# Reordering the softmax chunks and the scores of an attention and feed-forward kernel

## The chip, the core and the metric

The kernel runs as one program on one core of a Trainium2 chip. The metric is the device time of one execution in microseconds (us), as the median over the runs shown. Below, PE is TensorE (the matmuls), PEld its weight loads, DVE is VectorE, ACT is ScalarE, POOL is GpSimd and SP is SyncE, which issues most of the DMAs.

## What is computed

The inputs are x (2048 tokens of 512 numbers), the weights of a sliding-window attention with 32 heads of 16 numbers, and those of a gated feed-forward layer with 1792 hidden units. The reference, cut to what matters:

```
xn = layernorm(x)
q, k, v = split(xn @ wqkv)                       # 32 heads, 16 numbers each
mask = (0 <= idx[:, None] - idx[None, :] < 256)  # each token sees itself and 255 before it
p = softmax(where(mask, q k^T * 16**-0.5, -1e9))
s = (p v) @ wo
g = silu((silu(xn @ w1) * (xn @ w3)) @ w2)
return x + s * g
```

The kernel takes the maximum of every row first and subtracts it before the exponential. Products of two f32 matrices are made as three f16 products (high by high, low by high, high by low).

## The kernel before, in words

**Stages.** Tokens go in four tiles `t` of 512. Heads go in four groups `g` of eight, and a group in two halves `p` of four heads. A `(t, g, p)` is a unit; there are 32, and the outer loop (L1157) walks through them. In a unit PE makes, interleaved, four kinds of work:

- `pass1` (L542): scores with the queries on the partitions, eight parts for a unit (four blocks of 128 queries, two pairs of heads). Each writes one scores tile `s` (matmuls of L558), and DVE takes the maximum of each row (L568). It runs two units ahead of `pass2`. A unit's maxima are turned by two small matmuls (`finish`, L583) that write into spare columns of another part's scores tile, and go through a DMA into two rows of `qa`.
- `pass2` (L608): scores again, with the keys on the partitions and the maxima subtracted in the matmul (L629). This is done in chunks; the tuple `CHUNKS` (L64) lists them for tiles 1 to 3, `FIRST` (L70) for tile 0. A piece `(m, k, n, at, used)` is 64 keys from block `m` against `n` blocks of 64 queries. DVE adds masks (L636) and ACT takes the exponential into a tile `pt` (L639). The first two chunks of `CHUNKS` have 8 blocks of queries for each half of the keys and for one pair of heads each (`a` = 0, then 1), as pieces of 5 and 3; the next two the same in pieces of 5, 2 and 1; the last one has 4 blocks for both pairs of heads.
- the products with v (`values`, L643, L655): f32 matmuls of 64 rows by 32 columns, so that eight fit into the array beside each other (two halves of the keys by four heads). They come in two calls for a unit of tiles 1 to 3: chunks 0, 1, 2 and then chunks 3, 4 (`cuts`, L987). The two last units, which have no `pass1` beside them, make three calls: (0, 1), (2, 3) and (4).
- dense work: projections (L504), values (L471), the two products of the feed-forward layer (`gate_up` L797, `down` L842) and the output (L884). Each group of 9 or 12 matmuls fills one bank `m0` or `m1`, in two halves; the two banks alternate, and DVE or ACT empties a bank when its group is complete.

**What sets the order.** PE's order is the order of the program; the other engines' orders are made by the scheduler, with `urgent()` pieces ahead. `batches` (L981) lists the scores of a unit, `pass2`'s and `pass1`'s in turn, and takes them two at a time as a batch; after the two scores of a batch come the products with v that the batch before made ready (`late`). `spread` (L1015) puts dense pieces between the batches. A unit of tiles 1 to 3 has 5 + 8 = 13 scores, so one is carried into the next unit: in every other unit each batch has the weights' scores (`pass2`) first, in the ones between the maxima's scores (`pass1`) first. Scores tiles `s` come from a pool of two buffers; a buffer is free again when DVE has the maxima, or ACT the exponentials.

**Delayed steps.** `later(n, f)` runs `f` after `n` steps; a step is one dense piece or one batch. `later_in_bank` (L151) does the same for pieces that use a bank for a moment, but only in the middle of an open dense group (`pump`, L157), and takes the bank that is not open (`bank(short=True)`, L170).

**Scaling weights.** In tile 0 the raw weights are scaled to powers of two. `squares` (L221) sums squares on ACT and DVE, `powers` (L249) adds them over the partitions with a matmul with ones (L255) into such a bank, and DVE makes the power of two from it. Then `split` or `split_pool` cut the weights into f16 halves on ACT, DVE and POOL. `measure` (L737) does it for two slices of the feed-forward weights at once.

**The next tile's x.** `prepare_beside(t)` (L445) loads four blocks of x, takes their means and variances on DVE (`stats`, L371, from 8 steps later on), centres them, and turns them with small matmuls into spare columns of `pass1`'s scores tiles (`turn_beside`, L418, from the list `besides`).

Of the kernel before, what the change touches and what calls it, by code (L numbers as in the profile page):

```python
# [76 lines left out]
def tile_block(ctx: ExitStack, tc: tile.TileContext, x, wqkv, wo, w1, w3, w2, out):  # L77
# [50 lines left out]
    queue = []  # L128
    banked = []
    started = []  # L130
# [19 lines left out]

    def later_in_bank(n, f):  # L151


        made_so_far[0] += 1
        banked.append((now[0] + n, made_so_far[0], f))

    def pump():  # L157
        due = min((q for q in banked if q[0] <= now[0]), default=None)
        if due is not None:
            banked.remove(due)  # L160
            due[2]()

    def flush():
        while queue or banked:
            step()
            pump()

    open_bank = [0]

    def bank(shape, dtype=F32, short=False):  # L170

        b = 1 - open_bank[0]
        if not short:
            open_bank[0] = b
        return psm.tile(shape, dtype, name=f"m{b}", tag=f"m{b}", bufs=1)


# [70 lines left out]

    def powers(sb, n, p2, inv):  # L249


        ps = bank([P, n], short=True) if started else pss.tile([P, 2, 512], F32, name="s")[:, 0, 0:n]
        m = sb.shape[-1] // n
        for i in range(m):
            nc.tensor.matmul(ps, onesb, sb[:, i * n:(i + 1) * n], start=i == 0, stop=i == m - 1)  # L255
        al = small.tile([P, n], F32, name="al")
        nc.vector.tensor_scalar(al, ps, 2.08, 1e-30, op0=ALU.mult, op1=ALU.max)

        nc.vector.tensor_scalar(al.bitcast(I32), al.bitcast(I32), 24, 23, op0=ALU.logical_shift_right,
                                op1=ALU.logical_shift_left)  # L260
        nc.vector.tensor_scalar(p2, al, 2.0**63, None, op0=ALU.mult)
        nc.vector.reciprocal(inv, p2)

# [23 lines left out]
    def weights(name, w):  # L287

        cell = {}

        def load():
            cell["raw"] = [take(F32) for _ in range(NC)]
            for c, raw in enumerate(cell["raw"]):
                nc.sync.dma_start(raw, w[c * P:(c + 1) * P, :])

        def norm(apart=0):
            cell["sb"] = squares(cell["raw"], on_act=2 * (name == "wv"), apart=apart)

        def scale():
            p2 = const.tile([P, 1], F32, name=f"p2{name}")  # L300
            inv = const.tile([P, 1], F32, name=f"inv{name}")
            powers(cell["sb"], 1, p2, inv)
            cell["p2"], cell["inv"], cell["sw"] = p2, inv, scaled(inv, WS, f"sw{name}")

        def cut(apart=0):
            hi = const.tile([P, NC, D], F16, name=f"{name}h")
            lo = const.tile([P, NC, D], F16, name=f"{name}l")

            def one(c, raw):
                split(hi[:, c, :], lo[:, c, :], raw, cell["sw"])  # L310
                give(raw)
            for c, raw in enumerate(cell["raw"]):
                if apart:
                    later(apart * c, lambda c=c, raw=raw: one(c, raw))
                else:
                    one(c, raw)
            SQ[name] = hi, lo, cell["p2"], cell["inv"]
        return load, norm, scale, cut

    def weights_qk(g):  # L320
# [10 lines left out]

        def scale():
            p2 = const.tile([P, 1], F32, name=f"p2qk{g}")
            inv = const.tile([P, 1], F32, name=f"invqk{g}")
            powers(cell["sb"], 1, p2, inv)
            cell["p2"], cell["sw"] = p2, scaled(inv, WS, f"sw{g}")

# [23 lines left out]
    def prepare(t):  # L361
# [32 lines left out]
        def turn(b):  # L394
# [9 lines left out]
            else:  # L404
                pt = pss.tile([P, 2, 512], F32, name="s")[:, 0, :].rearrange("p (k q) -> p k q", q=P)
            for k in range(NC):
# [37 lines left out]

    def prepare_beside(t):  # L445

# [3 lines left out]
        for b in range(4):  # L450
            made.append((0, lambda b=b: later(8 + b, lambda: stats(b))))
        made.append((0, lambda: later(12, lambda: rstd(0, 4))))
        for b in range(4):
            made.append((0, lambda b=b: later(13 + b, lambda: centre(b))))
        return made, lambda: besides.extend(lambda s, b=b, n=n: turn(b, n, s) for b in range(4) for n in (0, 2))
# [22 lines left out]


    maxima = []  # L480
    besides = []
    QA = {}
# [59 lines left out]
    def pass1(t, g, p):  # L542
# [6 lines left out]
        def part(ii, a):  # L549
            qa, ka = QA[t, g], keys(t, g)  # L550
            i = t * 4 + ii
            n, mask = ((i + 1) * P, M1.rearrange("p a b -> p (a b)")[:, (1 - i) * P:]) if i < 2 else (WIN, MW)
            s = pss.tile([P, 2, 512], F32, name="s")
            for c in range(2):
                e = (ii + 3) * P if i < 2 else (ii + 2) * P + 64 * (c + 1)
                for r in range(2):
                    rows = slice(64 * r, 64 * r + KR)
                    nc.tensor.matmul(s[64 * c:64 * c + 64, r, :n], qa[rows, 2 * p + a, ii * P + 64 * c:ii * P + 64 * c + 64],  # L558
                                     ka[rows, 2 * p + a, e - n:e], start=True, stop=True)
# [38 lines left out]
    def last_maxima():  # L598
        s = pss.tile([P, 2, 512], F32, name="s")
        after = [f(s) for f in maxima]  # L600
# [7 lines left out]
    def pass2(t, g, p, cuts):  # L608
# [14 lines left out]
        def scores(c):  # L623
            qa, ka = QA[t, g], keys(t, g)
            s = pss.tile([P, 2, 512], F32, name="s")
            for o, h, a, (m, k, n, _, _) in pieces(c):
# [110 lines left out]
    def measure(f, apart=0):  # L737
# [3 lines left out]

        def scale():
            pp = small.tile([P, 3, 2], F32, name="pp")
            pi = small.tile([P, 3, 2], F32, name="pi")
            powers(sb, 6, pp.rearrange("p a b -> p (a b)"), pi.rearrange("p a b -> p (a b)"))
            ff = slice(f, f + 2)
# [234 lines left out]
    def batches(n, u, ahead):  # L981
# [9 lines left out]
        if u and not ahead and maxima:  # L991
            order.append((last_maxima, None))
        for k in range(max(len(rows1), len(rows2))):
            order += [(f, c) for f, c in zip(rows2[k:k + 1], cols2[k:k + 1])]
            order += [(f, None) for f in rows1[k:k + 1]]
        if len(order) % 2 and n < len(units) - 1:
# [3 lines left out]
        due = late_cost[0]  # L1000
        for pair in pairs:
            def batch(pair=pair):
                for f, _ in pair:
                    f()
                ready = late[:]
                late.clear()
                late.extend(c[1] for _, c in pair if c)
                for c in ready:
                    c()
            made.append((due, batch))  # L1010
            due = sum(COLS * c[0] for _, c in pair if c)
        late_cost[0] = due
        return made

    def spread(made, dense):  # L1015
# [4 lines left out]
        for k, (cost, batch) in enumerate(made):  # L1020
# [3 lines left out]
            while dense and (at + dense[0][0] / 2 <= whole * (k + 1) / len(made) or dense[0][0] == 0):  # L1024
                c, piece = dense.pop(0)
                at += c
                piece()
                if is_open([(c, piece)]):
                    pump()
                if c:  # L1030
# [3 lines left out]
    def run(dense):  # L1034
        for c, piece in dense:
            piece()
            if started and is_open([(c, piece)]):
                pump()
            if c:
# [32 lines left out]
    def keep_busy(n):  # L1072
        ps = bank([P, 4, P], short=True)
        for _ in range(n):
# [58 lines left out]
    later_in_bank(3, lambda: (qk[3][2](), later(2, qk[3][3])))  # L1133
    spread(batches(-1, None, units[1]), project(0, 2, 1) + project(0, 2, 0) + more(EARLY))

# [21 lines left out]
    for n, u in enumerate(units):  # L1157
        if n == 1:
            first, second = prepare_beside(1)
            run(first)  # L1160
            later(22, second)
        if n == 6:
            wout[0]()
        if n == 7:
            wout[1](2)
            later_in_bank(12, lambda: (wout[2](), later(2, lambda: wout[3](2)), later(3, out_scale)))
        want += a_unit - other[n]
# [8 lines left out]
    while late:  # L1176
# [4 lines left out]
        step()  # L1181
    while banked:
        step()
        pump()
    for b in range(2):
# [33 lines left out]
```

## Time and profile before

| | |
|---|---|
| median of 3 runs | 899.93 us (899.12 to 901.4) |
| the profiled execution | 900.77 us |
| its span, first to last instruction | 898.7 us |
| mean granted clock of TensorE | 0.992 of full speed |
| instructions in the span | 22393 |

The profiled execution took 2.07 us more than its span; this lies before the first and after the last instruction. Line numbers are those of the kernel before. In a line of the timeline the first number is the start in us from the start of the span, the second how long the group of equal instructions lasted, `x` how many there were, and the bracket how long the engine was idle before and who ended it. A matmul's listed end is modelled and reaches over the start of the next one, so distances are taken from start to start. In a line of the waits the numbers are us in total, how many times, and the longest.

### The profile page before, as it was taken

How to read it: one execution, taken by the hardware profiler on the slowest of the kernel's cores; microseconds unless marked ns; L12 is line 12 of the kernel's file. 1: busy time of each engine (PE TensorE's matmuls, PEld its weight loads, DVE VectorE, ACT ScalarE, POOL GpSimd, SP SyncE). 2: the span in 40 equal slices, each digit the busy share in tenths (PEclk: the TensorE clock that was granted, in tenths of full speed). 3: DMA queues.
4: the chain of work that ended last, by engine and by line, in shares of the span. 5: the costliest groups of instructions: out<-in, count | busy, mean ns of one | idle time of the engine just before them, and what ended most of it. 6: DMA issues, size and time to landing. Idle time of an engine off the chain costs nothing.

```text
span 898.7 us, 22393 instructions
## 1 busy us (share of the span) xinstructions
PE 848.7 (94%) x8695; PEld 391.5 (44%) x8695; DVE 613.2 (68%) x2009; ACT 407.4 (45%) x594; POOL 193.4 (22%) x317
## 2 busy tenths in 40 slices
PE   9797997889999999999999999999999999999997
PEld 4333443344444444444445444444444444444443
DVE  8676777766787676787668675766566676666435
ACT  6895866573425444233343444443343334442521
POOL 2244236251101102121111111121111112121211
PEclk9999899999999999999999999999999999999999
DMA  9865434547443344442432334333343243332301
GB/s 302 260 203 156 148 126 131 183 113 225 119 135 84 97 135 131 115 130 74 145 100 72 108 105 149 112 114 84 98 123 93 78 132 113 98 119 58 88 8 59
DMA packets 95322, 110.61 MB, mean 123 GB/s; under 512 B 17200, under 2 KB 60528, under 8 KB 95216
## 3 DMA queue, kind: packets, MB, share of 16 engines
q1 hardware_dynamic: 94928, 108.67, 41.0%
q8 instruction: 68, 1.11, 0.5%
q10 hardware_dynamic: 288, 0.52, 0.2%
q14 instruction: 38, 0.31, 0.1%
HBM read 76.28 MB, written 28.57 MB: 117 GB/s over the span
## 4 chain that ended last, share of the span: by engine, by line
PE 52%; DVE 15%; DMA 10%; issue 9%; ACT 7%; SPq 4%; POOL 3%; POOLq 0%; ACTq 0%; DVEq 0%
PE m L797 19%; PE m L842 9%; PE po L655 8%; DVE junk L568 5%; ACT pt L639 5%; PE m L504 3%; PE s L558 3%; DVE s L636 3%; PE s L629 3%; DMA slot<-in_B_w_dram 3%; PE m L471 3%; PE m L884 3%; POOL slot L276 2%; DMA dr<-dd 2%; SPq L702 2%
## 5 line engine op out<-in xcount | busy, mean ns | idle before, releaser
L639 ACT ACTIVATE pt<-s,es 128x1024 f32<-128x1024 f32 x152 | 169.1, 1115 | 252.2 <-DVE s L636 226.9
L568 DVE CUSTOM_DVE_ANT_0 junk<-s,MW 128x320 bf16<-128x320 f32 x448 | 217.9, 486 | 78.1 <-PE s L558 56.7
L797 PE MATMUL m<-XH,slot 128*128 128x512 f16 x896 | 268.7, 382 | 1.9 <-DVE slot L517 1.9
L276 POOL TENSOR_TENSOR slot<-slot,slot 128x256 f16<-128x256 f32 (+1 forms) x220 | 144.4, 681 | 543.7 <-ACT slot L821 391.0
L797 PEld LDWEIGHTS <-slot 128*128 128x128 f16 x1344 | 122.9, 98 | 155.2 <-issue 13.7
L797 PE MATMUL m<-XL,slot 128*128 128x512 f16 x448 | 170.3, 380 | 0.0
L842 PE MATMUL m<-slot,slot 128*128 128x512 f16 x672 | 157.6, 383 | 1.6 <-DVE slot L812 1.2
L636 DVE TENSOR_TENSOR s<-s,MK 128x256 f32<-128x256 f32 (+2 forms) x280 | 121.3, 435 | 40.9 <-PE s L629 37.0
L655 PE MATMUL po<-pt,V 64*32 64x320 f32 (+4 forms) x2880 | 100.8, 348 | 0.0
L842 PEld LDWEIGHTS <-slot 128*128 128x128 f16 x672 | 61.8, 98 | 83.1 <-issue 12.7
L558 PE MATMUL s<-KA,qa 48*64 48x320 f16 (+2 forms) x1024 | 73.3, 304 | 15.4 <-ACT pt L639 8.5
L655 PEld LDWEIGHTS po<-pt,V 64*32 64x32 f32 x2880 | 62.3, 106 | 34.1 <-issue 15.5
L629 PE MATMUL s<-qa,KA 50*64 50x320 f16 (+3 forms) x1472 | 61.7, 258 | 12.0 <-ACT pt L639 10.8
L629 PEld LDWEIGHTS <-KA 50*64 50x64 f16 x1472 | 37.1, 105 | 57.1 <-issue 37.1
L808 ACT ACTIVATE slot<-m,sgs 128x512 f32<-128x512 f32 x56 | 38.4, 686 | 50.2 <-PE m L797 49.0
L812 DVE SCALAR_TENSOR_TENSOR slot<-slot,m 128x512 f32<-128x512 f32 x56 | 38.4, 686 | 31.0 <-ACT slot L808 27.9
L817 DVE SCALAR_TENSOR_TENSOR slot<-m,slot 128x512 f32<-128x512 f32 x56 | 38.4, 685 | 29.2 <-PE m L797 28.9
L558 PEld LDWEIGHTS <-qa 48*64 48x64 f16 x1024 | 28.3, 105 | 67.2 <-issue 42.4
L821 ACT CAST slot<-slot 128x512 f16<-128x512 f32 x56 | 34.6, 617 | 47.4 <-DVE slot L817 46.8
L858 DVE SCALAR_TENSOR_TENSOR slot<-m,dsc,slot 128x512 f32<-128x512 f32 x48 | 35.9, 747 | 22.0 <-PE m L842 21.4
L276 POOL TENSOR_TENSOR on<-on,rb 128x256 f32<-128x256 f32 x32 | 23.0, 741 | 129.3 <-DMA dm<-mt 47.0
L504 PE MATMUL m<-XH,whi 128*128 128x512 f16 x120 | 44.8, 381 | 0.2 <-DVE slot L812 0.2
(143 smaller groups left out, 849.0 us busy)
## 6 DMA issues: line engine op xcount, KB each, us to landing
slot<-dW SPq DMA_DIRECT2D x126, 256.0 KB
slot<-in_B_w_dram SPq DMA_DIRECT2D x42, 256.0 KB
dW<-slot SPq DMA_DIRECT2D x42, 256.0 KB
slot<-in_A_x_dram SPq DMA_DIRECT2D x30, 256.0 KB
KA<-dK SPq DMA_DIRECT2D x24, 288.0 KB
qa<-dQ SPq DMA_DIRECT2D x32, 192.0 KB
dK<-slot SPq DMA_DIRECT2D x16, 256.0 KB
dQ<-slot SPq DMA_DIRECT2D x16, 256.0 KB
```

The source lines that it names most:

```text
L276: op(out[:, c], a[:, c], b[:, c])
L504: nc.tensor.matmul(cell["pp"], a[:, k, c, :], b[:, c, :], start=(c, i) == parts[0][0], stop=(c, i) == parts[-1][-1])
L558: nc.tensor.matmul(s[64 * c:64 * c + 64, r, :n], qa[rows, 2 * p + a, ii * P + 64 * c:ii * P + 64 * c + 64], ka[rows, 2 * p + a, e - n:e], ...
L568: nc.vector.tensor_tensor_reduce(out=junk[:, :n], in0=s[:, r, :n], in1=mask, scale=1.0, scalar=NEG, op0=ALU.add, op1=ALU.max, accum_out=M[ ...
L629: nc.tensor.matmul(s[64 * h:64 * h + 64, r, o:o + 64 * n], ka[rows, 2 * p + a, 64 * (m + 4):64 * (m + 5)], qa[rows, 2 * p + a, 64 * (m + k ...
L636: nc.vector.tensor_add(v, v, MK[:, kind, of:of + n, :].unsqueeze(1).to_broadcast([P, 2 * len(which), n, 64]))
L639: nc.scalar.activation(pt, s, AF.Exp, scale=es)
L655: nc.tensor.matmul(cell["po"][32 * i:32 * i + 32, h, 64 * (m + k):64 * (m + k + n)], V[64 * h:64 * h + 64, (4 * t + m // 2) % VB, hd * VW: ...
L797: nc.tensor.matmul(cell[k], w[:, (a * NC + c) * P:(a * NC + c + 1) * P], b[:, c, :], start=c == 0 and i == 0, stop=c == NC - 1 and i == 2)
L808: nc.scalar.activation(sg, cell[0], AF.Tanh, scale=sg_scale[:, f:f + 1])
L812: nc.vector.scalar_tensor_tensor(sg, sg, 1.0, cell[0], op0=ALU.add, op1=ALU.mult)
L842: nc.tensor.matmul(ps, hh[:, a * TW + b * P:a * TW + (b + 1) * P], w[:, c * D:(c + 1) * D], start=f == f0 and i == 0, stop=f == f1 - 1 and ...
```

## The change

Five things change together.

1. `CHUNKS`: the chunk of all four heads moves from the last to the first place. `cuts` stays, so for a unit of tiles 1 to 3 the first call of `values` now has that chunk and the two of pieces 5 and 3, and the second call the two of pieces 5, 2 and 1.
2. In every batch the weights' scores come first (`pair.sort`).
3. The matmuls with ones no longer use a dense bank. `powers` takes a scores tile of `pass1` and writes, as four 64 by 64 products, into its spare columns; a list `besides` says which part does it (`beside_scores`, in front of the turns of x). `later_in_bank`, `pump` and `short` go. DVE adds the two halves with one instruction more.
4. At most one part of a batch carries something in its spare columns (`alone`), save in tile 0 and the first group of tile 1.
5. For tile 1, `prepare_beside` does its statistics 6 steps later and gives the turns free after 26 steps in place of 22, and one projection (keys of tile 1, group 0) goes a unit later.

```diff
-CHUNKS = (*((a, ((0, 0, 5, 0, 1), (-2, 2, 3, 5, 1)), ((1, 0, 5, 0, 1), (5, 0, 3, 5, 1)),
+CHUNKS = (((0, 1), ((4, 0, 4, 0, 1),), ((-1, 1, 4, 0, 1),), ((0, 3, 2, 2, 0),)),
+          *((a, ((0, 0, 5, 0, 1), (-2, 2, 3, 5, 1)), ((1, 0, 5, 0, 1), (5, 0, 3, 5, 1)),
              ((0, 4, 2, 0, 0), (5, 2, 2, 1, 0))) for a in AB),
           *((a, ((2, 0, 5, 0, 1), (6, 0, 2, 5, 1), (-4, 4, 1, 7, 1)), ((3, 0, 5, 0, 1), (7, 0, 1, 5, 1), (-3, 3, 2, 6, 1)),
-             ((0, 4, 2, 0, 0), (5, 2, 2, 0, 0))) for a in AB),
-          ((0, 1), ((4, 0, 4, 0, 1),), ((-1, 1, 4, 0, 1),), ((0, 3, 2, 2, 0),)))
+             ((0, 4, 2, 0, 0), (5, 2, 2, 0, 0))) for a in AB))
...
-    def bank(shape, dtype=F32, short=False):
-
-        b = 1 - open_bank[0]
-        if not short:
-            open_bank[0] = b
+    def bank(shape, dtype=F32):
+
+        open_bank[0] = b = 1 - open_bank[0]
         return psm.tile(shape, dtype, name=f"m{b}", tag=f"m{b}", bufs=1)
...
+    def beside_scores(n, f):
+
+        later(n, lambda: besides.insert(0, f))
...
-    def powers(sb, n, p2, inv):
+    def powers(sb, n, p2, inv, s=None):
...
-        ps = bank([P, n], short=True) if started else pss.tile([P, 2, 512], F32, name="s")[:, 0, 0:n]
         m = sb.shape[-1] // n
-        for i in range(m):
-            nc.tensor.matmul(ps, onesb, sb[:, i * n:(i + 1) * n], start=i == 0, stop=i == m - 1)
...
+            for h in range(2):
+                for c in range(2):
+                    for i in range(m):
+                        nc.tensor.matmul(s[64 * c:64 * c + 64, h, WIN:WIN + n],
+                                         onesb[64 * h:64 * h + 64, 64 * c:64 * c + 64],
+                                         sb[64 * h:64 * h + 64, i * n:(i + 1) * n], start=i == 0, stop=i == m - 1)
...
-            made.append((0, lambda b=b: later(8 + b, lambda: stats(b))))
-        made.append((0, lambda: later(12, lambda: rstd(0, 4))))
+            made.append((0, lambda b=b: later(more + 8 + b, lambda: stats(b))))
+        made.append((0, lambda: later(more + 12, lambda: rstd(0, 4))))
...
-            after = [f(s) for f in maxima if (ii, a) != (0, 0)]
-            if after:
+            after = []
+            if alone[0] and maxima and (ii, a) != (0, 0):
+                after = [f(s) for f in maxima]
                 maxima.clear()
-            elif besides:
+            elif alone[0] and besides:
                 after = [besides.pop(0)(s)]
+            alone[0] = not after or t * NG + g <= NG
...
-        (later_in_bank if started else later)(5 if started else 9 if apart else 6, scale)
+        if started:
+            beside_scores(4, scale)
+        else:
+            later(9 if apart else 6, scale)
...
         for pair in pairs:
+
+            pair.sort(key=lambda x: x[2])
+
             def batch(pair=pair):
-                for f, _ in pair:
+                alone[0] = True
+                for f, _, _ in pair:
                     f()
...
-    later_in_bank(1, lambda: (qk[2][2](), later(1, qk[2][3])))
+    beside_scores(4, lambda s: then(s, qk[2][2](s), lambda: later(1, qk[2][3])))
...
-            if max(2 * k - 5, 0) == n:
+            if max(2 * k - 5 + (k == NG), 0) == n:
                 beside[n] += project(*tiles[k], 1)
...
-            first, second = prepare_beside(1)
+            first, second = prepare_beside(1, 6)
             run(first)
-            later(22, second)
+            later(26, second)
```

More of the change, by code (lines that the diff above doesn't have):

```diff
@@ L149, in step, with scores_bank @@
             due[2]()
[L151 to L161, printed above, removed]
     def flush():
-        while queue or banked:
+        while queue:
             step()
-            pump()
     open_bank = [0]
-    def bank(shape, dtype=F32, short=False):
-        b = 1 - open_bank[0]
-        if not short:
-            open_bank[0] = b
+    def bank(shape, dtype=F32):
+        open_bank[0] = b = 1 - open_bank[0]
         return psm.tile(shape, dtype, name=f"m{b}", tag=f"m{b}", bufs=1)
+    def scores_bank():
+        return pss.tile([P, 2, 512], F32, name="s")
+    maxima = []
+    besides = []
+    alone = [True]
+    def beside_scores(n, f):
+        later(n, lambda: besides.insert(0, f))
     identf = const.tile([P, P], F32, name="identf")
@@ L330, in norm, with scale, rest @@
             cell["sb"] = squares(cell["raw"], on_act=2)
-        def scale():
+        def scale(s=None):
             p2 = const.tile([P, 1], F32, name=f"p2qk{g}")
             inv = const.tile([P, 1], F32, name=f"invqk{g}")
-            powers(cell["sb"], 1, p2, inv)
-            cell["p2"], cell["sw"] = p2, scaled(inv, WS, f"sw{g}")
+            def rest():
+                cell["p2"], cell["sw"] = p2, scaled(inv, WS, f"sw{g}")
+            return then(s, powers(cell["sb"], 1, p2, inv, s), rest)
         def cut(ks=(1, 0)):
@@ L404, in turn @@
             else:
[L405 removed]
+                pt = scores_bank()[:, 0, :].rearrange("p (k q) -> p k q", q=P)
             for k in range(NC):
@@ L598, in last_maxima @@
     def last_maxima():
-        s = pss.tile([P, 2, 512], F32, name="s")
+        s = scores_bank()
         after = [f(s) for f in maxima]
@@ L624, in scores @@
             qa, ka = QA[t, g], keys(t, g)
-            s = pss.tile([P, 2, 512], F32, name="s")
+            s = scores_bank()
             for o, h, a, (m, k, n, _, _) in pieces(c):
@@ L1006, in batch @@
                 late.clear()
-                late.extend(c[1] for _, c in pair if c)
+                late.extend(c[1] for _, c, _ in pair if c)
                 for c in ready:
@@ L1010, in batches @@
             made.append((due, batch))
-            due = sum(COLS * c[0] for _, c in pair if c)
+            due = sum(COLS * c[0] for _, c, _ in pair if c)
         late_cost[0] = due
@@ L1072, in keep_busy @@
     def keep_busy(n):
-        ps = bank([P, 4, P], short=True)
+        ps = bank([P, 4, P])
         for _ in range(n):
@@ L1165, in tile_block @@
             wout[1](2)
-            later_in_bank(12, lambda: (wout[2](), later(2, lambda: wout[3](2)), later(3, out_scale)))
+            beside_scores(12, lambda s: then(s, wout[2](s), lambda: later(2, lambda: wout[3](2)), lambda: later(3, out_scale)))
         want += a_unit - other[n]
```

64 lines of the change are left out of this document (37 added, 27 removed).

## The prediction

> **What bounds the kernel now.** First the span on the profile's page, then busy time by stage (0:285 is tile 0, 285:830 tiles 1 to 3 with both passes side by side, 830 on the end).
>
> ```profile
> span 898.7 us, 22393 instructions
> ```
>
> ```profile
> 0.00:285.00 285.00, 257.35 (x2441) 115.90 (x2445) 209.62 (x776) 174.79 (x307) 89.68 (x163) 0.98 0.56 170
> 285.00:830.00 545.00, 527.69 (x5722) 246.04 (x5726) 372.17 (x1181) 211.93 (x260) 91.34 (x136) 1.00 0.37 108
> 830.00:898.70 68.70, 63.71 (x544) 29.51 (x536) 31.42 (x54) 20.65 (x27) 12.37 (x18) 0.99 0.18 51
> ```
>
> The columns behind the length are PE, PEld, DVE, ACT and POOL. In the middle stage PE is busy 527.69 of 545 us; DVE, the next engine, 372.17, or 68%. What is taken off PE there shortens the kernel almost one for one, and about 17 us of idle PE are the most that better order can win. In the first stage PE is idle 27.65 us (285 less 257.35), so there a wait can be won, but other engines are late as well. What PE waits for, by stage (middle first, then the first):
>
> ```profile
> PE s L629 <- ACT pt L639: 9.5, 19, 1.3
> PE s L558 <- ACT pt L639: 4.6, 8, 1.3
> ```
>
> ```profile
> PE m L255 <- DVE sb L242: 4.3, 1, 4.3
> PE m L255 <- DVE slot L817: 4.3, 1, 4.3
> PE m L255 <- DVE slot L812: 1.7, 1, 1.7
> PE m L255 <- DVE slot L517: 0.8, 1, 0.8
> ```
>
> In the middle the scores wait for the exponential that frees their tile; in tile 0 the largest waits stand before the products with ones (L255). The change touches all three: PE's products with v, the scores' waits, the products with ones.
>
> **Step 1, the chunks.** The timeline of PE shows the products with v of the first and the last unit whose calls are (0, 1, 2) and (3, 4), there being 22 such units (24 units of tiles 1 to 3 less the last two), each with the start of the next work:
>
> ```profile
> 288.58 1.96 PE L655 MATMUL po<-pt,V 64*32 64x320 f32 x56
> 290.48 0.39 PE L797 MATMUL m<-XH,slot 128*128 128x512 f16 x1
> ...
> 295.45 1.53 PE L655 MATMUL po<-pt,V 64*32 64x320 f32 x40
> 296.91 0.39 PE L797 MATMUL m<-XH,slot 128*128 128x512 f16 x1
> ...
> 809.28 1.96 PE L655 MATMUL po<-pt,V 64*32 64x320 f32 x56
> 811.17 0.39 PE L797 MATMUL m<-XH,slot 128*128 128x512 f16 x1
> ...
> 816.63 1.53 PE L655 MATMUL po<-pt,V 64*32 64x320 f32 x40
> 818.09 0.39 PE L797 MATMUL m<-XH,slot 128*128 128x512 f16 x1
> ```
>
> From start to start the first call takes 1.90 and 1.89 us, the second 1.46. The last two units show other sums of chunks, (0, 1), then (2, 3) with (4) right behind it, then (2, 3) alone, then (4) alone:
>
> ```profile
> 837.54 1.09 PE L655 MATMUL po<-pt,V 64*32 64x320 f32 x32
> 838.57 0.39 PE L797 MATMUL m<-XH,slot 128*128 128x512 f16 x1
> ...
> 843.12 1.69 PE L655 MATMUL po<-pt,V 64*32 64x320 f32 x64
> 844.74 0.39 PE L797 MATMUL m<-XH,slot 128*128 128x512 f16 x1
> ...
> 856.60 1.26 PE L655 MATMUL po<-pt,V 64*32 64x320 f32 x48
> 857.79 0.39 PE L842 MATMUL m<-slot,slot 128*128 128x512 f16 x1
> ...
> 863.72 0.66 PE L655 MATMUL po<-pt,V 64*32 64x256 f32 x16
> 864.32 0.39 PE L797 MATMUL m<-XH,slot 128*128 128x512 f16 x1
> ```
>
> Count the blocks of 64 queries that the busiest of the eight places of the array gets. The pair a = 0 has 8 in chunk 0, 8 in chunk 2 and 4 in chunk 4; a = 1 has 8 in 1, 8 in 3, 4 in 4. Call (0, 1, 2) gives 16 to a = 0 and 8 to a = 1; (3, 4) gives 12 to a = 1 and 4 to a = 0; (0, 1) gives 8 and 8; (4) gives 4 and 4. The times are 1.89, 1.46, 1.03 and 0.60: 0.43 us for 4 blocks, 0.17 fixed. So a call costs its fullest place, 0.1075 us a block, and the places with less stand empty. Only (2, 3) is dearer than its 8 blocks, 1.19 in place of 1.03; it is the call of pieces 5, 2 and 1 in all places.
>
> After the change the first call has 4 + 8 = 12 blocks in every place, of pieces 4, 5 and 3: 1.46. The second is today's (2, 3), the same matmuls in the same order: 1.19. A unit saves 1.895 + 1.46 - 1.46 - 1.19 = 0.705 us, 22 units 15.5. In the two last units, whose calls stay (0, 1), (2, 3), (4), it turns round: 12 + 8 + 8 blocks for 8 + 8 + 4. The one goes from 1.03 + 1.62 to 1.46 + 1.89 (the last two calls side by side, 16 blocks), the other from 1.03 + 1.19 + 0.60 to 1.46 + 1.19 + 1.19: together 1.7 more. **Sum: -13.8.** Bounds: -17 if the small pieces cost nothing, and the loss of the second rival below.
>
> **Step 2, the weights' scores first.** A batch of a unit that has them first (on PE, DVE and ACT), and three of a unit with the maxima's first:
>
> ```profile
> 592.95 0.41 PE L629 MATMUL s<-qa,KA 50*64 50x256 f16 x8
> ...
> 593.66 0.69 DVE L636 TENSOR_TENSOR s<-s,MK 128x512 f32<-128x512 f32 x1
> ...
> 594.39 1.12 ACT L639 ACTIVATE pt<-s,es 128x1024 f32<-128x1024 f32 x1
> ```
>
> ```profile
> 603.85 0.33 PE L558 MATMUL s<-KA,qa 48*64 48x320 f16 x4
> 604.76 0.41 PE L629 MATMUL s<-qa,KA 50*64 50x320 f16 x8 [0.57 <-ACT pt L639]
> 607.79 0.33 PE L558 MATMUL s<-KA,qa 48*64 48x320 f16 x4
> 607.96 0.20 PE L583 MATMUL s<-identh,NM 64*64 64x64 f16 x2
> 608.42 0.42 PE L629 MATMUL s<-qa,KA 50*64 50x320 f16 x12 [0.27 <-ACT pt L639]
> 611.46 0.33 PE L558 MATMUL s<-KA,qa 48*64 48x320 f16 x4
> 611.62 0.40 PE L629 MATMUL s<-qa,KA 50*64 50x320 f16 x12
> ```
>
> Where nothing waits (611.46), L629 starts 0.16 us behind L558. At 603.85 it starts 0.91 behind, 0.75 too late, and at 608.42 0.46 behind the turn of the maxima, some 0.4 too late: 1.15 for this unit. Maxima first means that DVE takes two maxima before it masks, the exponential starts later, and the next batch needs that tile. With the weights first, the scores' start to the exponential's end is 592.95 to 595.51, 2.56 us; the batches in these rows are 3.67 and 3.94 apart, and step 1 takes 0.43 from those that hold a first call, so 3.2 stays at the closest. There are 11 units of the kind with maxima first. Worth: at most 11 times 1.15 = 12.7. At the least, the 9.5 of the waits row, less another 4.6 if the maxima's scores (L558, now second in all units) wait twice as much as now: 4.9. **I take -9**, the middle, as both ends are worked out from one row or one unit.
>
> **Step 3, the products with ones in tile 0.** They lose their own wait for a dense bank. Rows around the largest such wait:
>
> ```profile
> 83.35 1.46 PE L842 MATMUL m<-slot,slot 128*128 128x512 f16 x6
> ```
>
> ```profile
> 85.16 0.69 DVE L373 BATCH_NORM_STATS2 st<-slot 128x6 f32<-128x512 f32 x1 [3.04 <-DMA slot<-in_A_x_dram]
> ...
> 88.36 0.67 DVE L817 SCALAR_TENSOR_TENSOR slot<-m,slot 128x512 f32<-128x512 f32 x1
> ```
>
> ```profile
> 89.11 2.72 PE L842 MATMUL m<-slot,slot 128*128 128x512 f16 x6
> ```
>
> DVE stood 3.04 us before the statistics of x, whose load had not landed; L817 came late behind it, the bank was not free, PE stood 4.3 us, and the six matmuls after it took 2.72 in place of 1.46. After the change that product needs no bank, and the statistics come 6 steps (some 8 us of PE work, a step being a half group like the 1.46 above or a batch) later: -4.3 and -1.26. Of the waits for L812 (1.7) and L517 (0.8) a rest of some 0.5 stays, since the next group needs the bank 1.3 us later: -2.0. The wait for `sb` (4.3) is not one for a bank: the sums of squares are late, and the product moves only six matmuls back: -1.3, with 3 left. That is -8.9 at most. At the least it is 0: tile 0 has 27.65 us of idle PE in all, and a PE that comes earlier may stand for the split weights instead. **I take -6**, two thirds, because the largest wait has its own cause removed.
>
> What is added: eight groups of four to sixteen small matmuls (L583's two stand with 0.20 us, most of it overlapped, so between 0 and 1.6 in all; I take 0.5), one more small DVE instruction each, and the statistics and one projection moved, whose work is the same. The scores tile that carries them is released later, as with L583 today. Nothing more is counted.
>
> **Sum against the profiled execution** (900.77 us): -13.8 - 9 - 6 + 0.5 = -28.3, so 872.5. The median of the runs shown is 0.84 lower, so **872** is a run's likely time.
>
> **Rivals.**
>
> *The waits in tile 0 only move, and half of step 2 comes back as waits of the maxima's scores.* 900.8 - 13.8 - 4.9 + 0.5 = 882.6. For it: 27.65 us of idle PE in tile 0 with many small causes. Against it: the 4.3 us have a plain cause.
>
> *Matmuls start strictly in the program's order.* In the new first call, the first matmuls of the chunk of all heads and of the next chunk want the same place; if the second held up all behind it, the call would need 20 blocks one after the other, 2.32 us, and step 1 would lose 22 times 0.155 (2.32 + 1.19 against 3.355), with the 1.7 some 5 us: 891. Against it: counted so, today's first call would need 21 blocks, 2.43 us, and the rows show 1.89. [...]
>
> *Slower: the weights' scores wait in every batch.* If the exponential of one batch always ended after the next batch's scores are due, each of the 22 units would wait like the one at 603.85, 1.15 us; the shorter products with v would only lengthen these waits. Then step 1 wins nothing but its 1.7 loss, step 2 costs 11 more units of 1.15 (+12.7), step 3 wins 6: 900.8 + 1.7 + 12.7 - 6 + 0.5 = 909.7. It decides where scores' start to exponential's end passes 3.2 us. Against it: 2.56 above, and the few waits of the units that already have the weights first.
>
> *All of it comes through*: -17 - 12.7 - 8.9 = 862.
>
> **How the numbers follow.** Forecast, 866 to 878: 0.57. The first rival, 878 to 886: 0.19. Better than 866: 0.15. Strict order, 887 to 895: 0.04. Slower, over 903: 0.03; near no change: 0.02. The range 861 to 884 leaves out some 2 in 10. About 0.3% (2.7 us) is what a measurement can tell from no change; faster by more than that 0.95, within it 0.02, slower 0.03.
>
> **What would show it.** Products with v of tiles 1 to 3 as 48 and 48 records a unit, 1.46 and 1.19 from start to start, and 28 blocks in the last two units; L629's wait for `pt` near 0 in the middle stage and L558's at most doubled; no wait before the products with ones but the first, of about 3 us; DVE no longer standing for x at 85 us. It is wrong if the first call takes over 1.6, if idle PE in the middle stage does not fall from 17, or if tile 0's end stays near 285.

## The result, and the profile after

The kernel after takes 889.87 us (median of 4 runs, 888.56 to 891.04), the kernel before 900.29 us beside it (4 runs, 899.12 to 901.4): a ratio of 0.9884, 95% interval 0.9862 to 0.9906. It is faster by 10.4 us. 872 was forecast, with a range of 861 to 884, so two fifths of the gain came.

The profiled execution of the kernel after took 890.89 us. Its span, and busy time by stage (columns as before):

```profile
span 888.9 us, 22513 instructions
```

```profile
0.00:285.00 285.00, 255.03 (x2434) 114.53 (x2435) 202.97 (x766) 171.35 (x304) 88.03 (x161) 0.96 0.57 170
285.00:830.00 545.00, 538.41 (x5869) 252.02 (x5868) 377.70 (x1209) 221.37 (x270) 94.59 (x142) 1.00 0.39 110
830.00:888.90 58.90, 54.02 (x433) 25.55 (x431) 25.99 (x44) 15.39 (x21) 9.51 (x15) 0.99 0.12 38
```

In the middle, idle PE fell from 17.3 to 6.6 us (545 less 538.41). In the first stage it rose, and the granted clock fell from 0.98 to 0.96. The timeline of PE shows the two calls of the products with v in the first unit that has two, and the first call in the last such unit, each with the start of the next work:

```profile
295.42 2.13 PE L680 MATMUL po<-pt,V 64*32 64x256 f32 x48
297.48 0.61 PE L828 MATMUL m<-XH,slot 128*128 128x512 f16 x2
...
302.46 1.26 PE L680 MATMUL po<-pt,V 64*32 64x320 f32 x48
303.65 0.60 PE L828 MATMUL m<-XH,slot 128*128 128x512 f16 x2
...
798.97 2.13 PE L680 MATMUL po<-pt,V 64*32 64x256 f32 x48
801.02 0.61 PE L828 MATMUL m<-XH,slot 128*128 128x512 f16 x2
```

The second call takes 1.19 us, as forecast. The first takes 2.06 (297.48 less 295.42), not 1.46. The same rows mark three stretches, with the starts of the prediction's rows for before:

| stretch | before | after | difference |
|---|---|---|---|
| start to the first such call (tile 0) | 288.58 | 295.42 | +6.84 |
| from there to the last unit's first call | 520.70 | 503.55 | -17.15 |
| from there to the end of the span | 89.42 | 89.93 | +0.51 |

Tile 0, where 5.5 us were to be won, lost 6.8. The middle won 17.15, and of what? Taken from start to start of PE's records in the middle stretch, with gaps counted apart, in us:

| kernel | stretch | products with v | weights' scores | idle |
|---|---|---|---|---|
| before | 520.7 | 70.5 | 31.1 | 16.8 |
| sort alone (e3) | 509.5 | 70.7 | 26.7 | 8.1 |
| after | 503.6 | 68.3 | 26.1 | 6.6 |
| after, in rounds (e5) | 496.6 | 55.9 | 26.3 | 10.0 |
| sort and rounds (e6) | 499.0 | 56.5 | 26.6 | 11.8 |
| in rounds, cast on POOL (e14) | 492.8 | 55.7 | 26.3 | 8.3 |

All other groups of PE's work stay within 2 us. From before to after, the products give 2.2 us, the waits 10.2, and the weights' scores themselves 5.0: also they ran slower where they stood second. In before a group of them right behind the maxima's scores or their turn takes 0.32 to 0.35 us from start to start, any other that the next work follows without a wait 0.22 to 0.28, nearly all of them 0.24. The waits of the stage 285 to 830 in the kernel after (us in total, times, longest):

```profile
PE s L581 <- ACT pt L664: 2.8, 6, 1.0
...
PE s L654 <- ACT pt L664: 1.0, 2, 0.5
```

L654 (L629 before) waits 1.0 us for an exponential where it was 9.5, and the maxima's scores (L581) 2.8 where they were 4.6: they did not wait more for being second.

In tile 0 the largest wait is new. The timelines of PE, ACT and POOL around it:

```profile
198.05 0.33 PE L581 MATMUL s<-KA,qa 48*64 48x320 f16 x4
202.39 0.48 PE L581 MATMUL s<-KA,qa 48*64 48x320 f16 x4 [4.02 <-ACT pt L664]
202.80 1.61 PE L680 MATMUL po<-pt,V 64*32 64x320 f32 x24
```

```profile
197.21 0.62 ACT L852 CAST slot<-slot 128x512 f16<-128x512 f32 x1
200.71 0.62 ACT L732 CAST O<-on 128x512 f16<-128x512 f32 x1 [2.87 <-POOL on L298]
201.23 1.11 ACT L664 ACTIVATE pt<-s,es 128x1024 f32<-128x1024 f32 x1
```

```profile
197.40 1.92 POOL L298 TENSOR_TENSOR slot<-slot,slot 128x256 f16<-128x256 f32 x3 [0.44 <-ACT slot L302]
199.27 1.40 POOL L298 TENSOR_TENSOR on<-on,rb 128x256 f32<-128x256 f32 x2
```

PE waits for an exponential (L664). It stands on ACT behind the cast of the normalised product with v (L732, in `normalise`), and that waits for POOL, which has three halves of split weights to do before it multiplies `on`. In before the exponential of this place stands ahead of the cast:

```profile
198.53 1.12 ACT L639 ACTIVATE pt<-s,es 128x1024 f32<-128x1024 f32 x1 [1.26 <-DVE s L636]
...
200.05 0.62 ACT L707 CAST O<-on 128x512 f16<-128x512 f32 x1
```

In after the exponential's own input had been there since 196.34, when DVE ended the mask:

```profile
196.05 0.29 DVE L661 TENSOR_TENSOR s<-s,MK 128x128 f32<-128x128 f32 x1
```

After the wait the product with v takes 1.87 us from start to start, where the same call takes 1.00 in before. The granted clock goes with it: windows of PE alone (length, busy, clock, DMA share, GB/s), first two of after, then one of before.

```profile
203.00:206.00 3.00, 3.00 (x36) 0.50 0.60 178
200.00:225.00 25.00, 22.61 (x211) 0.86 0.52 146
```

```profile
200.00:225.00 25.00, 25.00 (x269) 1.00 0.67 209
```

From that product to the next call's it is 17.48 us in after (202.80 to 220.28) and 14.76 in before (199.96 to 214.72), so the wait costs up to 2.7 us more behind it. The 17 profiles of this case part in the same way. The ten with a wait of 2.7 us or more at this place have a clock of 0.86 to 0.93 in the window 200 to 225, and tile 0 ends in them (the first call of the products in tile 1 starts) at 292.01 to 295.42 us. The seven without it have 1.00 there and end tile 0 at 285.99 to 291.80.

### The profile page after: what moved, and what is told of

Read it like the earlier page. It is cut to its first block, busy times and chain, and to the rows that moved or that the text cites. A ratio compares the mean times of both kernels' runs of the same rounds, so it can differ in the third digit from the quotient of the medians.

```text
span 888.9 us, 22513 instructions
## 1 busy us (share of the span) xinstructions
PE 847.5 (95%) x8734; PEld 392.1 (44%) x8734; DVE 606.7 (68%) x2017; ACT 408.1 (46%) x594; POOL 192.1 (22%) x317
## 4 chain that ended last, share of the span: by engine, by line
PE 64%; DVE 12%; issue 7%; ACT 5%; POOL 5%; DMA 4%; SPq 2%; POOLq 0%; ACTq 0%; DVEq 0%
PE m L828 23%; PE m L873 12%; PE po L680 8%; PE m L527 6%; POOL slot L298 4%; PE s L654 4%; DVE junk L593 4%; PE s L581 3%; PE m L497 3%; PE m L915 3%; ACT pt L664 1%; DVE s L661 1%; SPq L727 1%; ACT sqa L229 1%; DMA slot<-in_A_x_dram 1%
## 5 line engine op out<-in xcount | busy, mean ns | idle before, releaser
L664 ACT ACTIVATE pt<-s,es 128x1024 f32<-128x1024 f32 x152 | 168.9, 1112 | 233.6 <-DVE s L661 231.9
L581 PE MATMUL s<-KA,qa 48*64 48x320 f16 (+2 forms) x1024 | 73.2, 299 | 22.4 <-ACT pt L664 10.7
L654 PE MATMUL s<-qa,KA 50*64 50x320 f16 (+3 forms) x1472 | 62.3, 261 | 5.2 <-ACT pt L664 2.8
L654 PEld LDWEIGHTS <-KA 50*64 50x64 f16 x1472 | 31.6, 105 | 69.8 <-issue 43.2
L581 PEld LDWEIGHTS <-qa 48*64 48x64 f16 x1024 | 29.1, 106 | 52.9 <-issue 28.8
```

What stands on the lines that cost most here:

```text
L654: nc.tensor.matmul(s[64 * h:64 * h + 64, r, o:o + 64 * n], ka[rows, 2 * p + a, 64 * (m + 4):64 * (m + 5)], qa[rows, 2 * p + a, 64 * (m + k ...
L664: nc.scalar.activation(pt, s, AF.Exp, scale=es)
```

## The experiments

The first four take the change apart. In all, the time of the kernel before beside them is 900.8 to 902.0 us.

**e1: which of a call's chunks goes first.**

```diff
+            cs = sorted(cs, key=lambda c: len(chunks[c][0]))
             for group in zip_longest(*(pieces(c) for c in cs)):
```

> The changed kernel with one edit: within a call of the products with v, the chunk of all four heads is issued behind the others instead of ahead of them (same matmuls, same sums of blocks). In the changed kernel the first call takes 2.06 us where 12 blocks should take 1.46. Theory (what is issued second wants the place that is already taken, and holds up what is behind it, although all places get 12 blocks): the first call falls to 1.46, 22 units win 0.6 each, -13 us, a time near 877. Rival (the pieces of 4 and 3 blocks themselves, or the two pairs of heads in one chunk, cost more): the call stays near 2.06 and the time near 890.

890.39 us, ratio 0.9875 (0.9859 to 0.9891); the first call still takes 2.06. So which of the two chunks comes first is not what counts, and the first explanation fell as it was put.

**e2: the chunks of before, all else changed.**

```diff
-CHUNKS = (((0, 1), ((4, 0, 4, 0, 1),), ((-1, 1, 4, 0, 1),), ((0, 3, 2, 2, 0),)),
...
+          ((0, 1), ((4, 0, 4, 0, 1),), ((-1, 1, 4, 0, 1),), ((0, 3, 2, 2, 0),)))
```

> The changed kernel with the tuple of chunks of before. Products with v of 1.89 and 1.46 us again in place of 2.06 and 1.19: 22 units lose 0.1 each, the last two win some 1.4, so within 1.5 us of the changed kernel (889 to 892) if the chunks are worth nothing as they stand; 13 us slower (903) if they had brought what was forecast and something else took it back.

889.97 us, ratio 0.9874 (0.9851 to 0.9897): the same time as with the new chunks. Calls of 1.895 and 1.46 again, and 1.4 us less in the last two units. Step 1, as it was made, was worth nothing.

**e3: the sort alone.** The kernel before with only `pair.sort`.

> The kernel before with one edit: the weights' scores first in every batch. Theory: the middle stage (first product with v of 56 records to the last) shrinks by some 15 us, from 520.7 to 506, and tile 0 stays at its length (first such product near 288.6), so a time near 885. Rival (tile 0's loss of 7 us comes from the sort as well): 892.

887.57 us, ratio 0.984 (0.982 to 0.9859), so this one line wins more than the whole change. The waits of its stage 285 to 830:

```profile
PE s L558 <- ACT pt L639: 3.8, 7, 1.2
...
PE s L629 <- ACT pt L639: 0.5, 1, 0.5
```

**e4: the products with ones and the moved work alone** (items 3 to 5 of the change). The kernel after with the chunks of before and without the sort.

> The changed kernel with the chunks of before and without the sort: the products with ones beside the maxima's scores, the rule of one such part a batch, and the later statistics and projection of tile 1 are left of the change. Theory: tile 0 is longer by some 7 us (first product with v of 56 records near 295), the middle stage as before, a time near 907. Rival (tile 0's loss needs the sort or the chunks, whose scores meet it): tile 0 at or below 288.6 and a time at or below 900.

904.36 us, ratio 1.0031 (1.0012 to 1.005): this part by itself makes the kernel slower, and tile 0 ends at 294.07.

**e5 and e6: the order of the matmuls within a call.** Both calls have the same blocks in every place, so what is left is the order. In e5 the first pieces of the two one-pair chunks come first, then the four pieces of the chunk of all heads, then the pieces of three:

```diff
-            for group in zip_longest(*(pieces(c) for c in cs)):
-                for c, item in zip(cs, group):
+            one = [c for c in cs if len(chunks[c][0]) == 1]
+            rounds = [(c, i) for group in zip_longest(*(pieces(c) for c in one)) for c, i in zip(one, group)]
+            k = 2 * len(one)
+            rounds[k:k] = [(c, i) for c in cs if c not in one for i in pieces(c)]
+            for c, item in rounds:
```

> The changed kernel, but the first call's products with v are issued in rounds over the places: the first pieces of the two chunks of one pair (all four of their places), then the four pieces of the chunk of all heads, then the pieces of three. The same 48 matmuls, 12 blocks in each place. Theory (TensorE looks only a limited number of instructions ahead of the oldest unfinished one, so that the places named last in the program get their first work late): the first call takes 1.46 us instead of 2.06, 22 calls give 13 us, about 877. Rival (the array is full with 96 blocks side by side, or the pieces cost what they cost): the call stays at 2.06 and the time at 890.

881.94 us, ratio 0.9784 (0.9757 to 0.9812). The timeline of PE in e5, first unit with two calls:

```profile
292.87 1.53 PE L684 MATMUL po<-pt,V 64*32 64x320 f32 x48
294.33 0.60 PE L832 MATMUL m<-XH,slot 128*128 128x512 f16 x2
...
299.31 1.26 PE L684 MATMUL po<-pt,V 64*32 64x320 f32 x48
300.50 0.61 PE L832 MATMUL m<-XH,slot 128*128 128x512 f16 x2
```

1.46 and 1.19, by order alone. The products fall by 12.4 us in the middle, idle time rises by 3.4: the batches are shorter, and PE waits more for exponentials (6.3 us in the stage 285 to 830, 3.8 in after). So 8 of 13 came. e6 has the same chunks and rounds on e3:

> The kernel before, with two parts: the weights' scores first in every batch, and the chunks of the change with the products issued in rounds as in the run beside it; products with ones and all of tile 0 as before. If the limited look-ahead is right: first call 1.46, second 1.19, so 0.7 us less a unit than the run with the sort alone (887.6), less 1.4 for the last two units: about 874. If the array is full: 2.06 and 1.19 together as much as before, about 888. The end of tile 0 stays near 288 in both.

878.3 us, ratio 0.9746 (0.9714 to 0.9778). Tile 0 ends at 287.74; the products fall by 14.2 us against e3, idle time rises by 3.7.

**e9: one pair of heads behind the other.** e5, with all matmuls of one pair of heads ahead of the other's:

```diff
+            if t and len(cs) > 1:
+                rounds.sort(key=lambda x: 0 if x[1] is None else x[1][2])
             for c, item in rounds:
```

> The changed kernel in rounds (881.9 us), but in tiles 1 to 3 each call issues all matmuls of the first pair of heads before those of the second: 24 records of the one, then 24 of the other, the same blocks in the same eight places. If TensorE looks ahead as far as it likes, the first call stays at 1.46 us and the second at 1.19. If it looked ahead nearly not at all, they would be near 2.8 and 2.1. If it looks a limited number of instructions ahead (weight loads counted: some 32 to 56, by a count of which orders cost what so far), the first call takes 2.0 to 2.4 and the second 1.6 to 1.8, and the time is 881.9 + 22 (0.5 to 0.9 + 0.4 to 0.6), about 902 to 915.

897.96 us, ratio 0.9955 (0.9934 to 0.9976). The timeline of PE in e9:

```profile
294.51 2.09 PE L686 MATMUL po<-pt,V 64*32 64x320 f32 x48
296.53 0.60 PE L834 MATMUL m<-XH,slot 128*128 128x512 f16 x2
...
301.51 1.66 PE L686 MATMUL po<-pt,V 64*32 64x320 f32 x48
303.10 0.60 PE L834 MATMUL m<-XH,slot 128*128 128x512 f16 x2
```

2.02 and 1.59, where e5 has 1.46 and 1.19, and where starts strictly in the program's order would give 2.43 for the first (21 blocks, counted as in the prediction). So the first call lies between free and strict order, and both are near the times that the expectation gives for a limited look-ahead (2.0 to 2.4 and 1.6 to 1.8). That it is one is the author's reading of these times; how far it goes is not shown. The time was some 4 us below the expected 902, since the longer calls covered waits: idle PE over the whole span is 37.6 us in e9 (895.9 less 858.34 busy) and 46.0 in e5 (878.7 less 832.73).

**e7, e8, e10, e11, e12: what holds up tile 0.** e7 calls the cast later in the kernel after:

```diff
-        later(13, cut)
+        later(16, cut)
```

> The changed kernel with the cast of the normalised product with v to 16 bit called 16 steps behind instead of 13, so that on ScalarE it no longer stands ahead of the exponential and waits there for GpSimd. Theory: the wait of 4.02 us near 198 us goes, and with it the half clock behind it; tile 0 ends 4 to 6 us earlier (289 to 291 instead of 295.4), about 885. Rival (what is late there is late for other reasons, and another wait comes in its place): no change, 889 to 891.

888.52 us, ratio 0.9855 (0.9832 to 0.9879). The run tested nothing, as ACT's timeline shows:

```profile
198.52 0.62 ACT L732 CAST O<-on 128x512 f16<-128x512 f32 x1 [2.87 <-POOL on L298]
199.04 1.11 ACT L664 ACTIVATE pt<-s,es 128x1024 f32<-128x1024 f32 x1
```

The cast still stands ahead of the exponential. e8 undoes all of item 5 of the change in the kernel after:

```diff
-            if max(2 * k - 5 + (k == NG), 0) == n:
+            if max(2 * k - 5, 0) == n:
...
-            first, second = prepare_beside(1, 6)
+            first, second = prepare_beside(1)
...
-            later(26, second)
+            later(22, second)
```

> The changed kernel with the statistics of the next tile's x, its turning and its one moved projection at the steps of the kernel before; the products with ones stay beside the maxima's scores. If the moved work is what made tile 0 longer, its end comes back to about 288 and the time to 883. If it is the products with ones (what waits on ScalarE and VectorE behind them), the end stays near 295 and the time at 890; if the later statistics do win something, as the prediction had it, the wait at 85 us (3 to 4 us) comes back and the time is 892 to 895.

887.55 us, ratio 0.9844 (0.9815 to 0.9873). Tile 0 ends at 291.80; the wait at 198 is down to 0.76, but one of 3.0 stands at 158. Inconclusive in size: after, e1, e2, e5 and e9 have the same tile 0 and end it at 295.42, 293.99, 293.50, 292.87 and 294.51. e10 is the other side of it: e6 with only these three edits of the change.

> The run with the sort and the rounds (878.3 us; products with ones in dense banks as before), with only the next tile's statistics, its turning and the one projection later, as in the change. If the prediction read the wait of 4 us near 85 us rightly (VectorE stands for x, the bank comes late), that wait goes and tile 0 ends 3 to 6 us earlier than 287.7, about 874. Rival (the later work runs into the maxima and the split weights further on, as the run with these steps undone shows it with 2 us the other way): the wait near 85 goes, others of 4 us or more come at 150 to 200, the end stays at 287 to 291, and the time at 878 to 881.

885.55 us, ratio 0.9819 (0.9793 to 0.9844), 7 us more than e6; tile 0 ends at 293.56. Neither theory had that. DVE and PE in e10:

```profile
85.49 0.69 DVE L373 BATCH_NORM_STATS2 st<-slot 128x6 f32<-128x512 f32 x1 [3.42 <-DMA slot<-in_A_x_dram]
```

```profile
88.91 0.17 PE L255 MATMUL m<-sb,onesb 128*128 128x6 bf16 x1 [4.15 <-DVE slot L821]
```

The statistics that should come 6 steps later stand where they stood (85.16 in before), and PE's wait behind them is there as well. The expectation for e11 below puts this down to a queue that is behind; the kernel does not bear that out, as `step` (L142) runs every piece that is due. What the traces show is that DVE's instructions stand in the same order in e6 and e10 for the first 368 of them, up to 132 us: the scheduler, which makes DVE's order, left the statistics where they were. Why is not shown. The second of the four loads of x is issued at 81.25 to 82.53 us in before, after, e6, e8 and e10, so with this order DVE has to stand. The new wait of 4.02 us (at 198 us) is in e10 too. e11 has of the three edits only the projection, on e6, and e12 is e5 without it:

> The run with the sort and the rounds (878.3 us), with only the one projection of tile 1 a unit later, as in the change; statistics and turning as before. With later statistics, turning and projection together tile 0 ended 5.8 us later (293.6 instead of 287.7), while the statistics themselves stood on VectorE where they stood before (85.5 us), since each step takes one piece of work from a queue that is behind. Theory: the projection does it, by shifting which dense work stands beside which batch, so that on ScalarE the cast of the normalised product comes ahead of an exponential at 198 us: end of tile 0 at 293 to 294, about 885. Rival (the turning 4 steps later does it): end at 287 to 289, 878 to 879.

> The changed kernel in rounds (881.9 us), with only the one projection back in its unit. If the projection makes the wait of 4 us at 198 us, this wait goes, tile 0 ends near 289 to 291 instead of 293 to 295, about 878 to 880, near the fastest so far (878.3). If it is the later turning, the wait stays and the time is 881 to 883.

e11: 883.34 us, ratio 0.9804 (0.9768 to 0.984), tile 0 ends at 292.01, and the wait of 4.02 us is there (at 197 us). The projection is enough to make it. e12: 882.03 us, ratio 0.9782 (0.9748 to 0.9816), as e5; a wait of 2.71 us stays at 199, and there too the cast (199.87) stands ahead of the exponential (200.39). So the projection is one way to that order and not the only one.

**e13, e14, e15: the cast on POOL.** The three take the cast off ACT, in e11, e5 and e6:

```diff
-            nc.scalar.copy(o[:, 0, :], on)
+            for c in (slice(0, 256), slice(256, 512)):
+                nc.gpsimd.tensor_copy(o[:, 0, c], on[:, c])
             halves(nc.gpsimd.tensor_sub, o[:, 1, :], on, o[:, 0, :])
```

> The run with the sort, the rounds and the one projection a unit later (883.3 us, wait of 4.02 us at 197 us), with the cast of the normalised product with v on GpSimd in two halves instead of ScalarE, so that no exponential stands behind it. Theory (the exponential waits behind the cast, the cast for GpSimd): the wait falls under 0.8 us, the half clock behind it goes, tile 0 ends at 287 to 289 instead of 292.0, about 879. Rival (GpSimd or something else is late there whatever the order): the wait stays at 2.5 us or more and the time at 883.

> The changed kernel in rounds (881.9 us, end of tile 0 at 292.9, wait of 4.02 us at 197 us), with the same cast on GpSimd. Theory: that wait goes, the end comes to 288 to 290, about 878. Rival: the wait stays or another of its size takes its place, 881 to 883.

> The run with the sort and the rounds (878.3 us; there the exponential stands ahead of the cast), with the same cast on GpSimd. If the order on ScalarE alone matters: no change, 877 to 880. If the cast on GpSimd (two halves of about 0.65 us more a unit pair) holds up the halves of the weights behind it: 879 to 883.

e13: 874.18 us, ratio 0.9686 (0.9658 to 0.9715); the wait is 0.53, and tile 0 ends at 287.96. e14: 871.41 us, ratio 0.9669 (0.964 to 0.9699), the fastest of all; tile 0 ends at 285.99. e15: 875.81 us, ratio 0.971 (0.9685 to 0.9735), faster than "no change", but tile 0 ends at 290.84, 3.1 us later than in e6; the middle is 3.5 shorter and what follows it 1.8. What holds up its tile 0 is not shown. PE, ACT and POOL of e14 at the place:

```profile
195.82 0.33 PE L581 MATMUL s<-KA,qa 48*64 48x320 f16 x4 [0.52 <-ACT pt L664]
196.08 1.07 PE L684 MATMUL po<-pt,V 64*32 64x320 f32 x32
```

```profile
194.12 0.63 ACT L857 CAST slot<-slot 128x512 f16<-128x512 f32 x1
194.65 1.12 ACT L664 ACTIVATE pt<-s,es 128x1024 f32<-128x1024 f32 x1
```

```profile
196.20 1.42 POOL L298 TENSOR_TENSOR on<-on,rb 128x256 f32<-128x256 f32 x2
197.56 0.74 POOL L737 CAST O<-on 128x256 f16<-128x256 f32 x2
```

POOL reaches `on` as late as in the kernel after against the work around it, but no exponential waits for that: the order on ACT was the cause of this wait. Against e5, e14 wins 6.9 us in tile 0, 3.9 in the middle and 1.0 behind it. Of the 6.9, 5.1 lie between the call of the products ahead of the wait and the second one behind it (189.84 to 217.73 in e5, 188.07 to 210.84 in e14). Of the 3.9, 1.7 are idle time; whether the cast stood ahead of exponentials there too, or ACT merely has less to do, is not shown.

## Why the prediction was wrong, step by step

**Step 1 (-13.8 forecast, about -0.8 measured)** is the step that failed. The count of blocks by place was right for the work: e5 gives its 1.46 and 1.19, and there the products fall by 14.6 us in the middle (70.5 to 55.9) and cost 1.4 more in the last two units, near the forecast. It failed in the sentence "So a call costs its fullest place": with 12 blocks in each place the first call took 1.46, 2.06 or 2.02 us by its order alone (e5, after, e9). By its own sign (over 1.6 for the first call) it was wrong. In the changed order both the chunk of all heads and the next one begin with pair 0; that its places are behind for that, and the others' matmuls come too late in the program, is the author's reading of these three times. The rival of strict order (2.32) was as wrong as the free order (1.46); 2.06 lies between, and none of the cases had a call between the two. What makes it 2.06, in after and in e1 alike, is not shown. The loss in the last two units was right: 1.44 (6.90 us in five calls after, 5.46 before) for 1.7.

**Step 2 (-9 forecast)** was right in its mechanism and somewhat small. The median of e3 is 14.0 us below that of before beside it, and its profile 11.8 below the profile of before. The sort alone wins 11.2 us of the middle stretch: 8.7 of idle time and 4.4 in the weights' scores themselves, which the prediction did not price; 1.9 come back in other groups, most of it in the output product. Its worry that L558 would wait twice as much did not come true (4.6 before, 3.8 in e3). In the kernel after the two terms are 15.2.

**Step 3 (-6, and +0.5 added; +6.8 measured in this profile, +4.3 to +6.8 in the five of the same tile 0)** had the wrong sign. Two things failed. "The statistics come 6 steps (some 8 us of PE work) later" did not happen: DVE stands for x until 84 to 86 us in before, after, e6, e8 and e10 alike, in after like this:

```profile
84.26 1.29 DVE L399 BATCH_NORM_STATS2 st<-slot 128x6 f32<-128x512 f32 x2 [2.62 <-DMA slot<-in_A_x_dram]
```

So the later steps won nothing there. The waits of the products with ones for a dense bank did go, and the product with v that starts at 115.58 in before starts at 112.80 to 115.40 in the five. But a wait of 2.87 us for a bank came before a projection (at 128 us in after), and at 175 us before and after are level (175.10 and 175.13). The remark "a PE that comes earlier may stand for the split weights instead" was as near as the prediction came to the rest: an order on ACT that no view of before showed, with the cast ahead of the exponential. With the slower matmuls behind it (granted clock 0.50 from 203 to 206 us), it put the kernel after 5.6 us behind by the call at 220.28 (214.72 in before), and 1.3 more were lost up to the end of tile 0. Without that order, e14 ends tile 0 2.6 us before the kernel before, though its cast is on POOL, which before has not. Against e15, which has the cast on POOL as well and lacks items 3 to 5, it wins 4.9 us in tile 0 and 4.4 in the medians. So the step is worth some 3 to 5 us when the cast is out of its way, inside its bounds of 0 to 8.9.

Two numbers agree by chance. The 889.87 us lie where the prediction put strict order (887 to 895), but the call of 2.32 us that belongs to it did not come. And that 871.4 us is near the forecast 872 is chance in part: step 1 brought less, by the waits that came back, and the cast was no part of the change.

## What to carry to other kernels

In these runs packed small matmuls cost about their fullest place when the program named all places in turn (1.46 us for 12 blocks, 1.19 for 8 in small pieces), and more when it named one pair of heads behind the other (2.02 and 1.59 in e9), so write them in rounds over the places. When an edit shifts what stands beside what, look at what comes on its engine ahead of the instruction that PE waits for: in after a cast of 0.62 us stood 2.87 us for POOL ahead of an exponential, PE waited 4.02 us, and up to 2.7 us more went behind it. A call that came later in the program did not move the instruction on DVE, whose order the scheduler makes (85.49 us in e10, 85.16 in before), so look for the moved instruction in the trace before a gain is put on it.

## What the runs showed of the hardware that was not expected

Behind a wait of 4.02 us of PE the granted clock was 0.50 (203 to 206 us in after). The same 48 matmuls took 1.46, 2.06 or 2.02 us by their order alone (first call of e5, after and e9). The same tile 0 ended between 292.87 and 295.42 us in five profiled executions, so a difference of 2 us between two single profiles there shows nothing.
